# Earlier accumulating input transfers, four output slots, and a last half tile in two quarters

## The chip, the cores and the metric

The kernel runs on one core of a Trainium2 chip. The metric is the device time of one execution in microseconds. Seven executions of the kernel before gave a median of 156.28 us (155.72 to 157.04).

## The reference

The input x has 2048 rows and 640 columns in bf16. It is normalised per row; two branches read the result and their sum is added to x:

```python
x = A_x
xn = _layernorm(x, axis=-1)
return x + _A_ref(xn, A_w_r, A_w_i) + _B_ref(xn, B_w1, B_b1, B_w2, B_b2)
# _A_ref: irfft2(rfft2(xn) * (w_r + 1j * w_i)), over rows and columns
# _B_ref: gelu(xn @ w1 + b1) @ w2 + b2, inner width 1536
```

## The kernel before, in words

The rows are cut into 16 tiles (index c). Row 16p + c of x lies in partition p of tile c. Both branches are matrix products on TensorE. Branch A is a Fourier transform built from small tables: a forward part (tables gtab, etab, mtab), a filter multiplication on VectorE (L716, L721) with some small gathers into Zs (L731 to L738), and an inverse part (ntab, getab, htab). Branch B multiplies by W1, applies gelu on ScalarE into gT (L660), and multiplies by W2. All matmuls are issued by one helper, so they share line L477; copies out of PSUM share L484 (ScalarE) and L487 (VectorE).

The part that the change touches is the end. For a tile c, the output needs 24 matmuls of 320 columns for branch B (function second, two halves of the 640 columns), and two matmuls with htab for branch A, all summed in two PSUM banks. For the six tiles in STAGED (0, 2, 4, 6, 8, 10) the 24 matmuls run early; VectorE adds b2 and keeps the result as a float32 "kept sum" in the space of xnT (L795). For the other ten, ScalarE fills one of five float32 slots xo with b2 (L826), and the 24 and the two matmuls run together at the end. In both cases x itself is added by an accumulating DMA: GpSimd issues it at L828, and it adds a tile of x from DRAM to the kept sum or to the filled slot. VectorE then adds PSUM and that tile into a bf16 slot of ost (L840, one of three slots), and SP stores it (L842). Two tiles of branch A come from each inverse block of 16 matmuls with getab, whose result is copied to Wf (L484 or L487) and recombined by four VectorE instructions (L809, L814) before htab can be applied.

The order on each engine is not written by hand. The class Sched takes a list of operations with a cost, a priority, operands, "after" (a real dependency) and "gate" (only an order of planning: the operation is not planned before the gating one has started). It plans by greedy simulation; buffers taken from a Pool wait for the earlier users of their slot. For a DMA the plan adds a latency, of which lat is a part. sync() then turns dependencies into semaphore waits. Each engine executes its list in order, so an instruction that waits holds all behind it.

Two such rules sit on the input transfers: L826 has a gate, and L828 a dependency, on z_last (the last filter instruction) and on an output sum, os_ops[c - PACE] with PACE = 5. Tile 15, the last, is done in two halves, each with its own matmuls, sum and store.

Of the kernel before, what the change touches and what calls it, by code (L numbers as in the profile page):

```python
# [10 lines left out]
ALU = mybir.AluOpType  # L11

S = 2048
D = 640
F = 1536
H2 = 320
Q4 = 160
KP = 322
NFC = 12
# [104 lines left out]
PACE = 5  # L124
# [268 lines left out]
def bass_parallel_sum__spectral_gfnet__dense_activation_gelu__prompt_kernel(  # L393
# [13 lines left out]
    xv = A_x[0].rearrange("(p c) d -> p c d", c=16)  # L407
# [6 lines left out]
    K = Sched(nc, ["sp", "pe", "act", "dve", "pool"])  # L414
    with ExitStack() as es:
        def sb(name, shape, dtype=BF):
            return es.enter_context(nc.sbuf_tensor(name, shape, dtype))

        def view(t, off, dims):
            width = int(np.prod(t.shape[1:]))  # L420
            return bass.AP(tensor=t, offset=off, ap=[[width, 128]] + dims)
# [8 lines left out]
        htab = sb("htab", [128, 16, 128])  # L430
# [16 lines left out]
        TT = sb("T", [128, 11 * D])  # L447
        Zb = sb("Z", [128, 2, 4 * KP])
        Zs = sb("Zs", [128, 2, 2, 256])
        ost = sb("ost", [128, 3, D])  # L450
        xot = sb("xo", [128, 5, D], F32)
        PS = [es.enter_context(nc.psum_tensor(f"ps{i}", [128, 1024], F32)) for i in range(4)]

# [20 lines left out]
        def mms(lst):  # L474
            def f(e, _):
                for o_, lw, rh, st, sp_ in lst():
                    ins = e.matmul(o_, lhsT=lw, rhs=rh, start=st, stop=sp_)  # L477
                return ins
            return f
# [301 lines left out]
        def second(c, hs, fps, gate, done):  # L781
            part = list(gate)
            for f0 in range(0, NFC, 2):
                part = [K.op([("pe", 2 * len(hs) * mm_us(H2))], PRIO["fst" if done else "fin"] - c / 10, mms(lambda f0=f0: [
                    (ps(fps.slot + h, 0, H2), gT[:, fc, 128 * c:128 * c + 128], W2[:, fc, H2 * h:H2 * h + H2], fc == 0, done and fc == NFC - 1)
                    for fc in range(f0, f0 + 2) for h in hs]),
                    reads=B_w2s[f0 // 3:(f0 + 1) // 3 + 1] + [B_gT[block_of[c], fc] for fc in range(f0, f0 + 2)], writes=[fps], gate=part)]
            return part

        def halves(v):  # L790
            return v.rearrange("p (h n) -> p h n", n=H2)
        for i, c in enumerate(STAGED):
            fps, B_st2[c] = Buf(f"fst{c}", psum, 2, ZONE["fst"]), Buf(f"sum{c}")
            st_ops += second(c, (0, 1), fps, all_hps, True)
            K.op([("dve", dve_us(D))], 86, lambda e, _, i=i, fps=fps: e.tensor_tensor(  # L795
                out=halves(view(xnT, 2 * D * i, [[1, 2 * D]]).bitcast(F32)), in0=ps2(fps.slot, H2), in1=halves(b2bc[:]), op=ALU.add), reads=[fps, B_b2b], writes=[B_st2[c]], after=all_hps)
        for cp in range(8):
            yo, y2, yf = Buf(f"yo{cp}", p_yo), Buf(f"y2{cp}", p_y2), Buf(f"yf{cp}", p_yf)
            pr = PRIO["eps"] - cp / 5
            eps_ = [Buf(f"eps{cp}_{v}", psum, 2, ZONE["eps"]) for v in range(2)]  # L800
            K.op([("pe", FIVE)], pr, mms(lambda cp=cp, eps_=eps_: five(
                eps_, lambda g, n: V[:, (0, 2, 3, 1)[g], 2 * cp + n, :], lambda g, n: V[32 * g:32 * g + 32, 4, 2 * cp + n, :], getab)),
                reads=B_v + [B_ge], writes=eps_, gate=[fin_ops[2 * cp - 5]] if cp > 2 else [])
            for v in range(2):
                K.op([("act", act_us(640)), ("dve", dve_us(640))], pr,
                     copy(lambda v=v, yo=yo: view(Wf, YO + yo.slot * 2 * D + H2 * v, [[D, 2], [Q4, 2], [1, Q4]]),
                          lambda v=v, eps_=eps_: two(eps_[v])), reads=[eps_[v]], writes=[yo], after=filt_ops)
            for k, op in enumerate((ALU.add, ALU.subtract)):
                K.op([("dve", dve_us(D, 2))], pr + 2, lambda e, _, k=k, op=op, yo=yo, y2=y2: e.tensor_tensor(  # L809
                    out=view(Wf, Y2 + y2.slot * 2 * D + (H2 - 1) * k, [[H2, 4], [1 - 2 * k, Q4]]),  # L810
                    in0=view(Wf, YO + yo.slot * 2 * D, [[H2, 4], [1, Q4]]), in1=view(Wf, YO + yo.slot * 2 * D + Q4, [[H2, 4], [1, Q4]]), op=op),
                    port=True, reads=[yo], writes=[y2])
            for k, op in enumerate((ALU.add, ALU.subtract)):
                K.op([("dve", dve_us(D, 2))], pr + 3, lambda e, _, k=k, op=op, y2=y2, yf=yf: e.tensor_tensor(  # L814
                    out=view(Wf, YF + yf.slot * 2 * D + (D - 1) * k, [[D, 2], [1 - 2 * k, H2]]),
                    in0=view(Wf, Y2 + y2.slot * 2 * D, [[D, 2], [1, H2]]), in1=view(Wf, Y2 + y2.slot * 2 * D + H2, [[D, 2], [1, H2]]), op=op),
                    port=True, reads=[y2], writes=[yf])
            for n in range(2):
                c = 2 * cp + n
# [8 lines left out]
                K.op([("pool", 1.2)], 50, lambda e, _, c=c, xov=xov: e.dma_start(xov(0, D), xv[:, c, :], accum_op=ALU.add), reads=[xi], writes=[xo],  # L828
                     after=[z_last] + os_ops[max(c - PACE, 0):][:1], nbytes=163840, lat=1.0)
                part = []  # L830
                for hs in ((0, 1),) if c < 15 else ((0,), (1,)):
                    os_, fps = Buf(f"os{c}_{hs[0]}", p_os), Buf(f"fps{c}_{hs[0]}", psum, 2, ZONE["yps" if c in STAGED else "fps"])
                    a, b = H2 * hs[0], H2 * (hs[-1] + 1)
                    if c not in STAGED:
                        part = second(c, hs, fps, part + fin_gate(c), False)
                    fin_ops[c] = K.op([("pe", len(hs) * mm_us(H2))], PRIO["fin"] + 1 - c / 10, mms(lambda c=c, n=n, hs=hs, yf=yf, fps=fps: [
                        (ps(fps.slot + h, 0, H2), htab[:, c, :], view(Wf, YF + yf.slot * 2 * D + D * n + H2 * h, [[1, H2]]), c in STAGED, True) for h in hs]),
                        reads=[yf, B_h], writes=[fps], gate=part)
                    part = [fin_ops[c]]
                    os_ops.append(K.op([("dve", dve_us(H2 * len(hs)))], 95, lambda e, _, a=a, b=b, hs=hs, xov=xov, fps=fps, os_=os_: e.tensor_tensor(  # L840
                        out=halves(ost[:, os_.slot, a:b]), in0=ps2(fps.slot, H2)[:, hs[0]:hs[-1] + 1, :], in1=halves(xov(a, b)), op=ALU.add), reads=[fps, xi, xo], writes=[os_]))
# [33 lines left out]
```

## Time and profile before

| | |
|---|---|
| median of 7 executions | 156.28 us (155.72 to 157.04) |
| the profiled execution, its own time | 156.25 us |
| its span in the profile | 154.2 us |
| TensorE busy | 147.4 us (96%) |
| VectorE busy | 116.6 us (76%) |
| ScalarE busy | 86.6 us (56%) |
| GpSimd busy | 21.0 us (14%) |
| granted TensorE clock | 1.00 |

In the rows of the page, PE is TensorE's matmuls, PEld its weight loads, DVE VectorE, ACT ScalarE, POOL GpSimd and SP the engine that issues most transfers. A row of 40 digits cuts the span into slices of 3.85 us; a digit is the busy share in tenths. A wait is written "who <- whom: total us, times, longest us". A line of a timeline or of the chain gives its start in us from the beginning of the span, then its length. Matmuls overlap in the pipeline, so the distance from start to start is the better measure of what one costs.

### The profile page before, as it was taken

How to read it: one execution, taken by the hardware profiler on the slowest of the kernel's cores; microseconds unless marked ns; L12 is line 12 of the kernel's file. 1: busy time of each engine (PE TensorE's matmuls, PEld its weight loads, DVE VectorE, ACT ScalarE, POOL GpSimd, SP SyncE). 2: the span in 40 equal slices, each digit the busy share in tenths (PEclk: the TensorE clock that was granted, in tenths of full speed). 3: DMA queues.
4: the chain of work that ended last, by engine and by line, in shares of the span. 5: the costliest groups of instructions: out<-in, count | busy, mean ns of one | idle time of the engine just before them, and what ended most of it. 6: DMA issues, size and time to landing. Idle time of an engine off the chain costs nothing.

```text
span 154.2 us, 3728 instructions
## 1 busy us (share of the span) xinstructions
PE 147.4 (96%) x1525; PEld 101.0 (65%) x1533; DVE 116.6 (76%) x265; ACT 86.6 (56%) x177; POOL 21.0 (14%) x33
## 2 busy tenths in 40 slices
PE   5999999999999999999999999999999989999992
PEld 2499788999564545444557666766776757777770
DVE  3869999999974996798597699679579698762231
ACT  3199888988686788689786456349213053300000
POOL 1201121101200000000000000204643342210000
PEclk9999999999999999999999999999999999999999
DMA  4999928997999200413422000301999877942111
GB/s 105 330 362 395 292 70 171 208 171 110 159 176 226 34 0 4 122 9 128 128 30 104 0 4 0 66 23 54 215 265 271 225 195 191 240 97 75 55 43 43
DMA packets 20647, 20.80 MB, mean 135 GB/s; under 512 B 8088, under 2 KB 17304, under 8 KB 20504
## 3 DMA queue, kind: packets, MB, share of 16 engines
q1 hardware_dynamic: 18160, 15.30, 39.1%
q0 software_dynamic: 2304, 5.24, 15.3%
q8 instruction: 12, 0.20, 0.6%
q10 hardware_dynamic: 168, 0.04, 0.1%
q14 instruction: 3, 0.02, 0.1%
HBM read 13.69 MB, written 2.62 MB: 106 GB/s over the span
## 4 chain that ended last, share of the span: by engine, by line
PE 72%; DMA 12%; DVE 6%; SPq 2%; issue 2%; ACT 2%; POOL 1%; DVEq 0%; POOLq 0%; ACTq 0%
PE ps L477 72%; DMA XV<-in_A_x_dram 5%; DMA xnT<-in_A_x_dram 4%; DMA out_dram<-ost 3%; SPq L472 2%; DVE ost L840 2%; ACT Xb L484 1%; DVE stats L574 1%; ACT Wf L484 1%; DVE Wf L809 1%; POOL xo L828 1%; POOL xnT L828 1%; DVE Wf L487 0%; DVE T L593 0%; PE ps L602 0%
## 5 line engine op out<-in xcount | busy, mean ns | idle before, releaser
L477 PE MATMUL ps<-W,gT 128*128 128x320 bf16 x384 | 56.6, 299 | 0.5 <-DVE ost L840 0.4
L477 PE MATMUL ps<-xnT,W 128*128 128x256 bf16 (+2 forms) x412 | 55.4, 286 | 1.5 <-issue 0.6
L477 PEld LDWEIGHTS ps<-W,gT 128*128 128x128 bf16 x384 | 36.6, 98 | 15.8 <-DVE ost L840 1.2
L660 ACT ACTIVATE gT<-ps,b1col 128x256 bf16<-128x256 f32 (+2 forms) x84 | 40.0, 506 | 7.8 <-PE ps L477 5.3
L477 PEld LDWEIGHTS ps<-xnT,W 128*128 128x128 bf16 x420 | 34.7, 98 | 14.2 <-issue 1.3
L840 DVE TENSOR_TENSOR ost<-ps,xo 128x640 bf16<-128x640 f32 (+1 forms) x11 | 8.4, 764 | 12.5 <-PE ps L477 12.1
L484 ACT ACTIVATE Wf<-ps 128x640 bf16<-128x640 f32 x10 | 6.8, 701 | 18.9 <-PE ps L477 18.9
L574 DVE BATCH_NORM_STATS2 stats<-XV 128x6 f32<-128x320 bf16 x32 | 14.1, 469 | 2.5 <-DMA XV<-in_A_x_dram 2.4
L828 POOL DMA_DIRECT2D xnT<-in_A_x_dram x6 | 6.7, 1137 | 61.5 <-DVE Zs L486 57.0
L716 DVE TENSOR_TENSOR T<-Y,Wf 128x1288 bf16<-128x1288 bf16 x16 | 12.6, 828 | 1.0 <-ACT Y L484 0.4
L828 POOL DMA_DIRECT2D xo<-in_A_x_dram x10 | 10.4, 1088 | 19.3 <-DVE ost L840 15.8
L582 POOL TENSOR_TENSOR rstd<-ve,mhalf 128x2 f32<-128x2 f32 (+1 forms) x9 | 6.3, 703 | 33.0 <-DVE ve L581 33.0
L484 ACT ACTIVATE XV<-ps 128x640 bf16<-128x640 f32 x11 | 7.4, 703 | 5.0 <-PE ps L477 4.8
L484 ACT ACTIVATE Xb<-ps 128x640 bf16<-128x640 f32 x9 | 7.9, 896 | 3.7 <-PE ps L477 3.7
L487 DVE CAST Y<-ps 128x644 bf16<-128x644 f32 x8 | 6.6, 827 | 4.2 <-PE ps L477 4.0
L826 ACT ACTIVATE xo<-b2bc 128x640 f32<-128x640 bf16 x10 | 6.9, 734 | 3.3 <-DVE ost L840 3.3
L477 PE MATMUL ps<-etab,XW 128*128 128x160 bf16 (+1 forms) x128 | 8.6, 233 | 0.0
L477 PE MATMUL ps<-getab,XV 128*128 128x160 bf16 (+1 forms) x128 | 8.6, 233 | 0.0
L809 DVE TENSOR_TENSOR Wf<-Wf 128x640 bf16<-128x640 bf16 x16 | 7.2, 485 | 1.4 <-ACT Wf L484 1.3
L477 PEld LDWEIGHTS ps<-etab,XW 128*128 128x128 bf16 (+1 forms) x128 | 5.5, 95 | 3.8 <-DVE Y L487 0.7
L487 DVE CAST Xb<-ps 128x640 bf16<-128x640 f32 x7 | 6.2, 884 | 2.1 <-PE ps L477 2.1
L484 ACT ACTIVATE XW<-ps 128x640 bf16<-128x640 f32 x11 | 7.4, 700 | 0.5 <-PE ps L477 0.5
(49 smaller groups left out, 145.4 us busy)
## 6 DMA issues: line engine op xcount, KB each, us to landing
W<-in_B_w_dram SPq DMA_DIRECT2D x8, 480.0 KB, 4.5
xo<-in_A_x_dram POOLq DMA_DIRECT2D x10, 320.0 KB, 5.0
out_dram<-ost SPq DMA_DIRECT2D x15, 160.0 KB, 3.2
XV<-in_A_x_dram SPq DMA_DIRECT2D x7, 320.0 KB, 9.0
xnT<-in_A_x_dram POOLq DMA_DIRECT2D x6, 320.0 KB, 4.9
Wf<-in_A_w_r_dram SPq DMA_DIRECT2D x7, 160.5 KB, 4.4
Wf<-in_A_w_i_dram SPq DMA_DIRECT2D x7, 160.5 KB, 4.0
gtab<-c_G SPq DMA_DIRECT2D x1, 512.0 KB, 7.4
```

What stands on the lines that cost most here:

```text
L472: return K.op([(eng, cost)], 0, lambda e, _: e.dma_start(dst, src), reads=reads, writes=[buf], after=after, nbytes=nbytes, rate=rate)
L477: ins = e.matmul(o_, lhsT=lw, rhs=rh, start=st, stop=sp_)
L484: return e.activation(dst(), src(), ACT.Copy, scale=scale)
L487: return e.tensor_copy(dst(), src())
L574: K.op([("dve", 0.4)], 100 - c, lambda e, _, c=c, h=h: e.bn_stats(stats[:, c, 6 * h:6 * h + 6], view(XV, c * D + H2 * h, [[1, H2]])), read ...
L582: K.op([("pool", 0.75)], 100 - c, lambda e, _, a=a, b=b: e.tensor_tensor(out=rstd[:, a:b], in0=ve[:, a:b], in1=mhalf[:, 0:b - a], op=ALU.pow),
L660: K.op([("act", act_us(s1 - s0, 1))], pr + PRIO["gelu"], lambda e, _, s0=s0, s1=s1, fc=fc, hps=hps: e.activation(gT[:, fc, s0:s1], ps(hps. ...
L716: t_ops[pair].append(K.op([("dve", 0.05 + dve_us(4 * KP, 2))], pr, lambda e, _, k=k, Y=Y, TB=TB, pair=pair: e.tensor_tensor(out=view(TT, T ...
L809: K.op([("dve", dve_us(D, 2))], pr + 2, lambda e, _, k=k, op=op, yo=yo, y2=y2: e.tensor_tensor(out=view(Wf, Y2 + y2.slot * 2 * D + (H2 - 1 ...
L826: K.op([("act", act_us(640))], 30, lambda e, _, xov=xov: e.activation(xov(0, D), b2bc[:], ACT.Copy), reads=[B_b2b], writes=[xi], gate=[z_l ...
L828: K.op([("pool", 1.2)], 50, lambda e, _, c=c, xov=xov: e.dma_start(xov(0, D), xv[:, c, :], accum_op=ALU.add), reads=[xi], writes=[xo], aft ...
L840: os_ops.append(K.op([("dve", dve_us(H2 * len(hs)))], 95, lambda e, _, a=a, b=b, hs=hs, xov=xov, fps=fps, os_=os_: e.tensor_tensor(out=hal ...
```

## The change

The transfer at L828 loses its dependencies on z_last and on an earlier output sum: it waits only for the kept sum or the filled slot that it adds to. The filling at L826 keeps z_last as its gate alone. The planned latency of the transfer rises from 1.0 to 2.5. ost gets a fourth slot. Tile 15 is done as one half and two quarters of 160 columns; second and the loop take pieces (PSUM bank, first column, end column) instead of halves. The planner makes new orders for the end of each engine's list from this: on GpSimd the transfers of tiles 0, 2, 4 come first, then 1, 3, 5, 6, 7, 9, 8, and so on; TensorE's list differs from about 99 us on.

```diff
-        ost = sb("ost", [128, 3, D])
+        ost = sb("ost", [128, 4, D])
...
-        p_yo, p_y2, p_yf, p_xo, p_os = Pool(3), Pool(2), Pool(3), Pool(5), Pool(3)
+        p_yo, p_y2, p_yf, p_xo, p_os = Pool(3), Pool(2), Pool(3), Pool(5), Pool(4)
...
+        WHOLE = ((0, 0, H2), (1, H2, D))
+
+        def second(c, pcs, fps, gate, done):
+
             part = list(gate)
             for f0 in range(0, NFC, 2):
...
+                    (ps(fps.slot + k, 0, b - a), gT[:, fc, 128 * c:128 * c + 128], W2[:, fc, a:b], fc == 0, done and fc == NFC - 1)
+                    for fc in range(f0, f0 + 2) for k, a, b in pcs]),
...
                 if c not in STAGED:
                     K.op([("act", act_us(640))], 30, lambda e, _, xov=xov: e.activation(xov(0, D), b2bc[:], ACT.Copy), reads=[B_b2b], writes=[xi],
-                         gate=[z_last] + os_ops[max(c - PACE, 0):][:1])
-                K.op([("pool", 1.2)], 50, lambda e, _, c=c, xov=xov: e.dma_start(xov(0, D), xv[:, c, :], accum_op=ALU.add), reads=[xi], writes=[xo],
-                     after=[z_last] + os_ops[max(c - PACE, 0):][:1], nbytes=163840, lat=1.0)
+                         gate=[z_last])
+                K.op([("pool", 1.2)], 50, lambda e, _, c=c, xov=xov: e.dma_start(xov(0, D), xv[:, c, :], accum_op=ALU.add), reads=[xi], writes=[xo], nbytes=163840, lat=2.5)
                 part = []
-                for hs in ((0, 1),) if c < 15 else ((0,), (1,)):
-                    os_, fps = Buf(f"os{c}_{hs[0]}", p_os), Buf(f"fps{c}_{hs[0]}", psum, 2, ZONE["yps" if c in STAGED else "fps"])
-                    a, b = H2 * hs[0], H2 * (hs[-1] + 1)
+                for pcs in (WHOLE,) if c < 15 else (((0, 0, H2),), ((0, H2, H2 + Q4),), ((0, H2 + Q4, D),)):
+                    a, b = pcs[0][1], pcs[-1][2]
+                    os_, fps = Buf(f"os{c}_{a}", p_os), Buf(f"fps{c}_{a}", psum, len(pcs), ZONE["yps" if c in STAGED else "fps"])
...
-                    os_ops.append(K.op([("dve", dve_us(H2 * len(hs)))], 95, lambda e, _, a=a, b=b, hs=hs, xov=xov, fps=fps, os_=os_: e.tensor_tensor(
-                        out=halves(ost[:, os_.slot, a:b]), in0=ps2(fps.slot, H2)[:, hs[0]:hs[-1] + 1, :], in1=halves(xov(a, b)), op=ALU.add), reads=[fps, xi, xo], writes=[os_]))
+                    os_ops.append(K.op([("dve", dve_us(b - a))], 95, lambda e, _, a=a, b=b, xov=xov, fps=fps, os_=os_: e.tensor_tensor(
+                        out=ost[:, os_.slot, a:b] if b - a < D else halves(ost[:, os_.slot, :]), in0=ps(fps.slot, 0, b - a) if b - a < D else ps2(fps.slot, H2),
+                        in1=xov(a, b) if b - a < D else halves(xov(a, b)), op=ALU.add), reads=[fps, xi, xo], writes=[os_]))
```

In the changed file the lines of the input transfer, the output sum and its store are L831, L842 and L845; the filling is L829 and the kept sum L798.

More of the change, by code (lines that the diff above doesn't have):

```diff
@@ L778, in fin_gate @@
             return ([fin_ops[rest[i - AHEAD]]] if i >= AHEAD else st_ops[:]) + hps_ops[block_of[c]]
-        def second(c, hs, fps, gate, done):
+        WHOLE = ((0, 0, H2), (1, H2, D))
+        def second(c, pcs, fps, gate, done):
             part = list(gate)
             for f0 in range(0, NFC, 2):
-                part = [K.op([("pe", 2 * len(hs) * mm_us(H2))], PRIO["fst" if done else "fin"] - c / 10, mms(lambda f0=f0: [
-                    (ps(fps.slot + h, 0, H2), gT[:, fc, 128 * c:128 * c + 128], W2[:, fc, H2 * h:H2 * h + H2], fc == 0, done and fc == NFC - 1)
-                    for fc in range(f0, f0 + 2) for h in hs]),
+                part = [K.op([("pe", 2 * sum(mm_us(b - a) for _, a, b in pcs))], PRIO["fst" if done else "fin"] - c / 10, mms(lambda f0=f0: [
+                    (ps(fps.slot + k, 0, b - a), gT[:, fc, 128 * c:128 * c + 128], W2[:, fc, a:b], fc == 0, done and fc == NFC - 1)
+                    for fc in range(f0, f0 + 2) for k, a, b in pcs]),
                     reads=B_w2s[f0 // 3:(f0 + 1) // 3 + 1] + [B_gT[block_of[c], fc] for fc in range(f0, f0 + 2)], writes=[fps], gate=part)]
@@ L793, in bass_parallel_sum__spectral_gfnet__dense_activation_gelu__prompt_kernel @@
             fps, B_st2[c] = Buf(f"fst{c}", psum, 2, ZONE["fst"]), Buf(f"sum{c}")
-            st_ops += second(c, (0, 1), fps, all_hps, True)
+            st_ops += second(c, WHOLE, fps, all_hps, True)
             K.op([("dve", dve_us(D))], 86, lambda e, _, i=i, fps=fps: e.tensor_tensor(
@@ L834, in bass_parallel_sum__spectral_gfnet__dense_activation_gelu__prompt_kernel @@
                     if c not in STAGED:
-                        part = second(c, hs, fps, part + fin_gate(c), False)
-                    fin_ops[c] = K.op([("pe", len(hs) * mm_us(H2))], PRIO["fin"] + 1 - c / 10, mms(lambda c=c, n=n, hs=hs, yf=yf, fps=fps: [
-                        (ps(fps.slot + h, 0, H2), htab[:, c, :], view(Wf, YF + yf.slot * 2 * D + D * n + H2 * h, [[1, H2]]), c in STAGED, True) for h in hs]),
+                        part = second(c, pcs, fps, part + fin_gate(c), False)
@@ L838, in bass_parallel_sum__spectral_gfnet__dense_activation_gelu__prompt_kernel @@
+                    fin_ops[c] = K.op([("pe", sum(mm_us(hi - lo) for _, lo, hi in pcs))], PRIO["fin"] + 1 - c / 10, mms(lambda c=c, n=n, pcs=pcs, yf=yf, fps=fps: [
+                        (ps(fps.slot + k, 0, hi - lo), htab[:, c, :], view(Wf, YF + yf.slot * 2 * D + D * n + lo, [[1, hi - lo]]), c in STAGED, True) for k, lo, hi in pcs]),
                         reads=[yf, B_h], writes=[fps], gate=part)
                     part = [fin_ops[c]]
-                    os_ops.append(K.op([("dve", dve_us(H2 * len(hs)))], 95, lambda e, _, a=a, b=b, hs=hs, xov=xov, fps=fps, os_=os_: e.tensor_tensor(
-                        out=halves(ost[:, os_.slot, a:b]), in0=ps2(fps.slot, H2)[:, hs[0]:hs[-1] + 1, :], in1=halves(xov(a, b)), op=ALU.add), reads=[fps, xi, xo], writes=[os_]))
+                    os_ops.append(K.op([("dve", dve_us(b - a))], 95, lambda e, _, a=a, b=b, xov=xov, fps=fps, os_=os_: e.tensor_tensor(
+                        out=ost[:, os_.slot, a:b] if b - a < D else halves(ost[:, os_.slot, :]), in0=ps(fps.slot, 0, b - a) if b - a < D else ps2(fps.slot, H2),
+                        in1=xov(a, b) if b - a < D else halves(xov(a, b)), op=ALU.add), reads=[fps, xi, xo], writes=[os_]))
```

## The prediction

> **What bounds the kernel now.** I read the page first, then the waits, the chain in order of time, and the timelines of TensorE, VectorE and GpSimd around the places that these named. The page:
>
> ```profile
> span 154.2 us, 3728 instructions
> ...
> PE 147.4 (96%) x1525; PEld 101.0 (65%) x1533; DVE 116.6 (76%) x265; ACT 86.6 (56%) x177; POOL 21.0 (14%) x33
> ...
> DMA  4999928997999200413422000301999877942111
> ```
>
> TensorE is busy for 96% of the span, so only its gaps and its two ends can be shortened. The DMA row, slices counted from 0, is near zero in 22 to 27 (about 85 to 108 us) and seven to nine in 28 to 34: the accumulating input transfers come in a crowd. Who waits for whom:
>
> ```profile
> POOL xo L828 <- DVE ost L840: 15.8, 6, 7.8
> ...
> DVE ost L840 <- DMA xnT<-in_A_x_dram: 3.3, 3, 1.9
> ...
> PE ps L477 <- DVE ost L840: 0.4, 1, 0.4
> ```
>
> GpSimd sits for the output sum of an earlier tile before it issues an input (the wait that the change removes), VectorE for three late inputs; TensorE is charged with only 0.4 us. Of these only TensorE's own wait costs time. Its timeline gives it a place:
>
> ```profile
> 117.15 0.43 PE L477 MATMUL ps<-Wf,htab 128*128 128x320 bf16 x2
> 117.43 1.07 PE L477 MATMUL ps<-getab,XV 128*128 128x160 bf16 x16
> 118.33 0.43 PE L477 MATMUL ps<-Wf,htab 128*128 128x320 bf16 x2
> 118.83 3.43 PE L477 MATMUL ps<-W,gT 128*128 128x320 bf16 x24
> 122.10 0.43 PE L477 MATMUL ps<-Wf,htab 128*128 128x320 bf16 x2
> 122.38 1.07 PE L477 MATMUL ps<-getab,XV 128*128 128x160 bf16 x16
> 123.28 0.43 PE L477 MATMUL ps<-Wf,htab 128*128 128x320 bf16 x2
> 124.16 3.43 PE L477 MATMUL ps<-W,gT 128*128 128x320 bf16 x24 [0.44 <-DVE ost L840]
> ```
>
> Starts are what counts: 26 matmuls of 320 columns take 122.38 - 118.83 = 3.55 us, 136 ns each; an inverse block (getab) takes 0.90. Two matmuls should take 0.27, but 118.33 to 118.83 is 0.50 and 123.28 to 124.16 is 0.88: 0.23 and 0.61 us lost. The chain says why in the second case:
>
> ```profile
> 118.04 0.75 DVE ost L840
> 118.79 0.02 issue
> 118.80 4.14 DMA out_dram<-ost
> 122.94 0.33 issue
> 123.28 0.84 DVE ost L840
> 124.11 0.05 issue
> 124.16 27.00 PE ps L477 x216
> ```
>
> An output store took 4.14 us to land, the sum of tile 5 had to wait for its slot of the three in ost, and tile 7's matmuls for the PSUM that this sum frees. In the first case tile 3's sum (117.96 to 118.78 on VectorE) ran behind the recombinations of an inverse block that TensorE began at 114.06, in the midst of tile 3's matmuls. From 124.16 to the last matmul there is no gap.
>
> **What the Trainium skill says.** SBUF — State Buffer, "Who interferes with whom": a VectorE copy or tensor_scalar in a two-port mode and a GpSimd instruction lock each other out for a whole instruction; tensor_tensor does not lock out descriptor writing. The trace agrees with the second half: five issues from 106.13 on kept a pitch of 0.90 us beside pairs of L809/L814 that took 0.88 to 0.89 with or without them. For the first half there is one hint: the issue at 97.33 beside the last Zs copy (97.20 to 97.42) took 1.04 us instead of 0.88. DMA: Bandwidth & Descriptors, "Specifications": under 512 B a transfer is read, modified and written; nothing before shows a 320 B store. TensorE: Matmul & The Clock Gate, "LDWEIGHTS (loading the stationary operand)": a load takes columns/1.2 ns, 107 for 128; the trace has 98, yet full-height 160-column matmuls with their own loads start 69 to 70 ns apart, so the loads overlap.
>
> **The change part by part.**
>
> 1. Wait for z_last and an earlier output sum removed from L828. The six kept sums end at 86.5, 91.6, 96.2, 100.3 and later; GpSimd starts some 0.3 us after a release (as 119.07 after a sum ended 118.78). So the first issues move from 97.33 to about 86.8, 91.9 and 96.5, and the inputs of tiles 1, 3, 5, 6, 7, 9 follow between 97.4 and 103, before their old crowd at 106 to 117. Landing is 3.7 to 7.4 us in the old crowd; each input now lands over 5 us before its sum. VectorE's 3.3 us of input waits go.
>
> 2. ost with four slots. Tile 5's sum then waits for the store of tile 4's sum, issued near 113, not of tile 3's. The landing of 4.14 us has 9 us to hide in.
>
> 3. TensorE's order is replanned from 99 us. I followed it with the old durations. After the block that starts at 98.68 the same work remains up to tile 7's first matmul, in both orders: 140 matmuls of 320 columns x 0.136 = 19.04, six inverse blocks x 0.91 = 5.46: 98.68 + 24.50 = 123.18. The old kernel was there at 124.16: 0.98 of stalls, namely 0.09 at 101.6 (the second inverse block behind VectorE's copy of the first), 0.06 at 105.5, 0.23, 0.61. In the new order the 0.09 stays: first inverse block at 100.31, its copy on VectorE 101.42 to 102.24, the second could start at 102.31 but starts about 0.16 after that copy, 102.40. Then I looked for new waits. Tile 0's output matmul at 104.40: recombination ends 104.1. Tile 2's at 108.30: 108.0 (0.14 spare with the 0.16 of delay). Tile 4's at 111.83: 111.4. The inverse block of 114.06 now comes before all of tile 3's matmuls (at 112.92), so recombinations end by 117.2 and tile 3's sum follows its matmuls at once: 117.57 to 118.39, tile 5's first matmul due 118.55: 0.11 spare. Tile 5's sum: 122.29 to 123.11, tile 7's matmul due 123.27: 0.11 spare. So tile 7 starts at 123.27 instead of 124.16: **-0.89**. The spare 0.11 repeats in the later pairs, which had no gap before with the same pattern.
>
> 4. Fillings of xo (L826) lose their gates. On ScalarE they now stand ahead of the copies: the first runs while ScalarE idles (96.05 to 97.06); three run from 97.45 at a pitch of 0.63, and the copy behind them, on which the first inverse block waits, ends at 100.04, before 100.31. Later each filling waits for an output sum with an inverse copy queued behind it: tile 11's waits for tile 1's sum (113.94), so the copy at 114.03 starts at 114.61 and recombinations end near 117.2, for a block due 118.28. Covered by 1 us. Had sums waited for inputs again, this queue would pass it to TensorE.
>
> 5. Last half in quarters. 13 x 136 ns = 1.77 become 26 x 69.5 = 1.81: **+0.04**. The last sum has 160 columns: 640 take 0.82, 320 take 0.49, so 160 take 0.33: **-0.16**. The store has half the bytes; its 8 packets per DMA engine took 31 to 35 ns each, so at most -0.13, or a rise of about as much if a 320 B write is dearer. I take -0.03, bounds -0.13 and +0.3. The added store issue (0.33 on SP) falls 0.9 us before the last one and is hidden; unhidden it would cost 0.33.
>
> 6. GpSimd against the Zs copies. The issues at 91.9 and 96.5 (0.88 each), and the next one right behind it at 97.4, fall on VectorE's Zs copies at 92.4 and 97.06, which feed TensorE's blocks at 93.97 and 98.01. No run shows the copy as the loser. Bounds: 0, or all copies kept for a whole issue. One issue's rest (0.35) leaves about 0.1 to 0.25 on TensorE after spare. I take **+0.1**, since only GpSimd was seen to yield.
>
> Sum: -0.89 + 0.04 - 0.16 - 0.03 + 0.10 = -0.94. The profiled execution was 156.25 us for a span of 154.2; span 153.2, time 155.3. The median was 156.28, practically the same, so against it -0.6%.
>
> **The rivals.**
> - *A new wait replaces the old one* (inputs or GpSimd were never TensorE's limit; the spare of 0.11 is not there). For it: the margins are a tenth of a microsecond. Against: pairs after 124 ran this pattern without a gap. Most of 0.89 would come back: 156.0.
> - *Port lock, moderate:* the copies at 97.06 wait for two issues, about 0.9 late; 0.5 of spare at 98.01, then the queue of item 4 behind it: 0.4 to 0.5 lost, 155.7.
> - *Port lock, full; slower.* Place: the five Zs instructions between 92.4 and 98. Price: if each waits for a whole issue of 0.88, 4.4 us, less 0.5 spare and the gain of 1.04: 159.1. It decides from three such waits on (2.6 - 0.5 - 1.04 is a loss of 1.1). Against it: only three issues lie there, and queued copies need to lose once each.
> - *The store of 320 B rows is dear:* +0.3, 155.6.
> - *The change does nothing:* excluded for the order, since tile 5's wait for the late store is gone by construction.
>
> **How the numbers follow.** Forecast as summed (155.0 to 155.6): 0.56. Moderate lock or dear store (155.6 to 155.8): 0.17. New wait (155.8 to 156.5): 0.15. Full lock: 0.08; something unseen and slower: 0.04. About half a per cent, 0.78 us, is what a measurement tells from no change: faster means under 155.50, slower over 157.06. The forecast has four parts in five under 155.50, the mild cases a few hundredths more: 0.51 faster; 0.36 same; 0.13 slower. The range 154.9 to 156.4 leaves out the slower cases and a sliver of the rest.
>
> **What would show it.** Right: issues at L831 from about 87 us; the DMA row filled in slices 22 to 27 and thinner after 28; no VectorE wait for an input; TensorE 0.50 and 0.88 back at 0.27; last matmuls near 150.3; the last sum near 0.33 us. Wrong: TensorE gaps at 94 or 98 behind Zs with copies longer than 0.23 us (the lock), gaps behind L842 or ScalarE copies after 112 (a new wait), or more than 2.6 us from the last sum to the end (the store).

## The result, and the profile after

The median went from 156.28 us (33 runs) to 154.83 us (154.31 to 156.66, 13 runs): a ratio of 0.9902, 95% interval 0.9884 to 0.992. Ratios are formed over the fast executions alone (the 156.66 us is a slow one, with a granted clock of 0.989) and are not simply the quotient of the two medians. The profiled execution took 154.94 us, with a span of 152.8 us against 154.2. The direction was forecast; the gain was half as large again as the forecast: the median is 0.47 us below the predicted 155.3 and just below the low end of the range, 154.9.

The page of the kernel after, the lines that answer to the three of before:

```profile
span 152.8 us, 3751 instructions
...
PE 147.0 (96%) x1538; PEld 101.7 (67%) x1546; DVE 117.0 (77%) x267; ACT 86.3 (56%) x176; POOL 21.0 (14%) x33
...
DMA  3999936979989100224404043299865346551111
```

The DMA row, near zero in slices 22 to 27 before, now has two to four in 23 to 25 and nine in 26 and 27; in 28 to 34, where it had seven to nine, it has eight in the first and three to six in the others: the crowd of input transfers came forward. The waits of the kernel after:

```profile
POOL xnT L831 <- DVE xnT L798: 61.1, 6, 46.5
...
ACT xo L829 <- DVE ost L842: 19.1, 5, 5.8
POOL xo L831 <- ACT xo L829: 18.7, 6, 3.8
DVE ost L842 <- PE ps L477: 13.4, 12, 2.7
```

GpSimd waits only for what it adds to, the kept sum or the filled slot, and its first issues are these:

```profile
87.10 1.04 POOL L831 DMA_DIRECT2D xnT<-in_A_x_dram  x1 [46.48 <-DVE xnT L798]
92.14 0.88 POOL L831 DMA_DIRECT2D xnT<-in_A_x_dram  x1 [4.00 <-DVE xnT L798]
96.79 0.88 POOL L831 DMA_DIRECT2D xnT<-in_A_x_dram  x1 [3.77 <-DVE xnT L798]
```

The output sum waits for TensorE and for nothing else: the 3.3 us in which it waited for inputs are gone, and so is TensorE's wait for it. TensorE at the two places that the prediction named:

```profile
118.45 0.43 PE L477 MATMUL ps<-Wf,htab 128*128 128x320 bf16 x2
118.73 3.42 PE L477 MATMUL ps<-W,gT 128*128 128x320 bf16 x24
121.99 0.43 PE L477 MATMUL ps<-Wf,htab 128*128 128x320 bf16 x2
122.26 1.07 PE L477 MATMUL ps<-getab,XV 128*128 128x160 bf16 x16
123.17 0.43 PE L477 MATMUL ps<-Wf,htab 128*128 128x320 bf16 x2
123.44 2.74 PE L477 MATMUL ps<-W,gT 128*128 128x320 bf16 x19
```

The two distances that were 0.50 and 0.88 us are 118.73 - 118.45 = 0.28 and 123.44 - 123.17 = 0.27. The chain of work that ended last:

```profile
92.37 58.09 PE ps L477 x561
150.46 0.02 issue
150.48 0.32 DVE ost L842
```

One unbroken piece of TensorE from 92.37 us to the last sum. In the kernel before, the chain ended with

```profile
151.18 0.49 DVE ost L840
```

From the end of the last sum to the end of the span it is now 152.8 - 150.81 = 2.0 us; before it was 154.18 - 151.67 = 2.5 us. That last difference is what the forecast did not have.

The accounts of the two profiled executions, from the starts of TensorE's matmuls and the ends of the last sums and stores:

| term | forecast | measured |
|---|---|---|
| TensorE's gaps between 100 and 125 us | -0.89 | -0.98 |
| the last 26 matmuls of 160 columns instead of 13 of 320 | +0.04 | +0.04 |
| the last sum | -0.16 | -0.17 |
| the last store, issue to landing (1.58 to 1.50) | -0.03 | -0.08 |
| Zs copies beside GpSimd's issues | +0.10 | 0.00 |
| SyncE's stop at the end of its list | not in the sum | -0.43 |
| x loads 0.27 later at the start of this execution | none | +0.27 |
| sum | -0.94 | -1.35 |

The measured sum agrees with the difference of the spans, 152.8 - 154.2 = -1.4. It compares two single executions; how much its first row changes from one execution of the old order to another, the experiments show.

The row on SyncE comes from its own instruction records. SyncE closes the program by waiting for all output stores, up to two semaphores per wait instruction, and then takes a branch. Start in us and what it is, the last ones before the branch:

```
before (17 stores, 8 waits)              after (18 stores, 9 waits)
152.46  wait 6                           151.58  wait 6
152.53  wait 7                           151.65  wait 7
153.30  wait 8, on the last store        152.15  wait 8  (its store had landed at 151.42)
153.79  branch                           152.35  wait 9, on the last store
                                         152.41  branch
```

When nothing holds SyncE, one wait follows the next within 0.06 to 0.10 us. In the kernel before there are 0.49 us between the last wait, which ended when the last store had landed (153.28), and the branch: this is what the table calls SyncE's stop. In the kernel after the same 0.5 us lie between waits 7 and 8, while the last store is still under way (it landed at 152.33), and the branch follows the last wait by 0.06 us. Nothing in the diff speaks of this; the experiments had to say what moved it.

### The profile page after: what moved, and what is told of

It is laid out like the page before. It is cut to its first block, busy times and chain, and to the rows that moved or that the text cites. A ratio compares the mean times of both kernels' runs of the same rounds, so it can differ in the third digit from the quotient of the medians.

```text
span 152.8 us, 3751 instructions
## 1 busy us (share of the span) xinstructions
PE 147.0 (96%) x1538; PEld 101.7 (67%) x1546; DVE 117.0 (77%) x267; ACT 86.3 (56%) x176; POOL 21.0 (14%) x33
## 4 chain that ended last, share of the span: by engine, by line
PE 86%; DMA 5%; SPq 3%; DVE 2%; ACT 1%; issue 1%
PE ps L477 86%; DMA XV<-in_A_x_dram 5%; SPq L472 3%; ACT Xb L484 1%; DVE stats L574 1%; DVE T L593 0%; PE ps L602 0%; DVE xnT L487 0%; DVE ost L842 0%; DVE mv L576 0%
## 5 line engine op out<-in xcount | busy, mean ns | idle before, releaser
L477 PE MATMUL ps<-W,gT 128*128 128x320 bf16 (+1 forms) x396 | 56.6, 295 | 0.0
L477 PEld LDWEIGHTS ps<-W,gT 128*128 128x128 bf16 x396 | 37.4, 98 | 14.3 <-issue 0.8
L842 DVE TENSOR_TENSOR ost<-ps,xo 128x640 bf16<-128x640 f32 (+2 forms) x12 | 8.6, 713 | 12.4 <-PE ps L477 12.4
L829 ACT ACTIVATE xo<-b2bc 128x640 f32<-128x640 bf16 x10 | 7.1, 731 | 19.1 <-DVE ost L842 19.1
L831 POOL DMA_DIRECT2D xnT<-in_A_x_dram x6 | 5.4, 901 | 61.1 <-DVE xnT L798 61.1
L831 POOL DMA_DIRECT2D xo<-in_A_x_dram x10 | 9.5, 1042 | 18.7 <-ACT xo L829 18.7
```

Of the source, the lines that this page charges most:

```text
L842: os_ops.append(K.op([("dve", dve_us(b - a))], 95, lambda e, _, a=a, b=b, xov=xov, fps=fps, os_=os_: e.tensor_tensor(out=ost[:, os_.slot, ...
```

## The experiments

Two questions. **First, the TensorE gaps**: is it the early start of the inputs, the order of work, or the fourth slot of ost that closes them? **Second, the end**: why did 0.43 us go there? For the second there are two theories. A: the stop sits at a fixed place of SyncE's instruction list, 25 instructions from its first output store (17 stores and 8 waits in the kernel before, 18 stores and 7 waits in the kernel after); what counts is the one store more, not the quarters. B: the stop belongs to the end of the list, or to the last store. All ratios below are against runs of the kernel before on the same chip.

### One half left whole, quarters alone, slots alone, three slots

The first four were run together. e1_halves is the changed kernel with tile 15 in two halves again:

```diff
-                for pcs in (WHOLE,) if c < 15 else (((0, 0, H2),), ((0, H2, H2 + Q4),), ((0, H2 + Q4, D),)):
+                for pcs in (WHOLE,) if c < 15 else (((0, 0, H2),), ((0, H2, D),)):
```

> The changed kernel with tile 15 in two halves again; all else as changed. Theory 1 (the gaps of TensorE make the gain, the quarters bring only a shorter last sum, 0.17, and a slightly shorter store, 0.08, less 0.04 of matmuls): 0.2 us slower than the changed kernel, 155.05 us, ratio to before 0.992, and no gap of TensorE from 99 us on. Theory 2 (the end after the last sum, 2.5 us before and 2.0 us after, is 0.5 shorter because of the quarters): 155.5 us, ratio 0.995, with 2.5 us from the last sum to the end of the span.

155.53 us, ratio 0.9965 (0.9943 to 0.9986). The chain of this run:

```profile
92.02 58.13 PE ps L477 x548
150.16 0.02 issue
150.18 0.49 DVE ost L842
```

TensorE has no gap but one of 0.09 us, before the matmul at 102.33, and yet more than half of the gain is missing. From the end of the last sum, 150.67, to the end of the span it is 2.5 us again, and SyncE's branch comes 0.49 us after its last wait (152.32, 152.81), as before.

e2_quarters_only has the pieces of the changed kernel, with the waits of L826 and L828 and the three slots of before:

```diff
-                for hs in ((0, 1),) if c < 15 else ((0,), (1,)):
+                for pcs in (WHOLE,) if c < 15 else (((0, 0, H2),), ((0, H2, H2 + Q4),), ((0, H2 + Q4, D),)):
```

> The kernel before with tile 15 in a half and two quarters, nothing else. Theory 1: the gaps at 118 and 123 us stay, the end is 0.2 us shorter: 156.1 us, ratio 0.9987. Theory 2: 0.65 us shorter: 155.65 us, ratio 0.996, with 2.0 us from the last sum to the end.

155.36 us, ratio 0.9932 (0.991 to 0.9953). The part that the prediction priced at -0.15 us brought 0.81 us of median. Not all of that need be the quarters': in the profiled execution TensorE's gaps come to 0.19 us only, where the kernel before had 0.98 with the same waits. Its span ends 2.0 us after the last sum; the stop lies between wait 7 (152.49) and wait 8 (152.98), and the branch follows the last wait by 0.07 us.

e3_four_slots_only is the kernel before with four slots in ost:

```diff
-        ost = sb("ost", [128, 3, D])
+        ost = sb("ost", [128, 4, D])
...
-        p_yo, p_y2, p_yf, p_xo, p_os = Pool(3), Pool(2), Pool(3), Pool(5), Pool(3)
+        p_yo, p_y2, p_yf, p_xo, p_os = Pool(3), Pool(2), Pool(3), Pool(5), Pool(4)
```

> The kernel before with four slots of ost, nothing else. Theory 1: the gap of 0.61 us (tile 5's sum behind a store that lands late) goes, the gaps of 0.23, 0.09 and 0.06 stay: 155.7 us, ratio 0.996. Rival (the input that lands late holds that sum in any case): 156.2 us, ratio 1.0, with the gap still there and a VectorE wait for an input.

155.64 us, ratio 0.998 (0.9958 to 1.0002). Gaps of 0.84 us in all stay, against 0.98. The end of the chain of this run:

```profile
113.69 1.11 issue
114.81 5.10 DMA xnT<-in_A_x_dram
119.91 1.27 issue
...
123.74 0.75 DVE ost L843
124.53 27.00 PE ps L477 x216
```

No store stands in it. A late input does: the transfer into xnT took 5.10 us, the sum that uses it came after it, the recombinations on VectorE behind that, and the gap is still there. In this execution the slot was not the limit. The ratio lies between the two expectations and decides nothing: the interval holds both 0.996 and 1.0.

e4_three_slots is the changed kernel with three slots:

```diff
-        ost = sb("ost", [128, 4, D])
+        ost = sb("ost", [128, 3, D])
...
-        p_yo, p_y2, p_yf, p_xo, p_os = Pool(3), Pool(2), Pool(3), Pool(5), Pool(4)
+        p_yo, p_y2, p_yf, p_xo, p_os = Pool(3), Pool(2), Pool(3), Pool(5), Pool(3)
```

> The changed kernel with three slots of ost; the order of all engines stays as changed. Theory 1 (inputs moved forward leave the stores a quiet time, so that a store lands within 3 us and three slots suffice): as the changed kernel, 154.85 us, ratio 0.990. Rival (the fourth slot carries the 0.61): 155.45 us, ratio 0.9945, with a gap of TensorE before tile 7.

154.68 us, ratio 0.9906 (0.9874 to 0.9938): the changed kernel within its interval, with no TensorE gap. Once the inputs come early, the fourth slot brings nothing that shows. In the medians of this group the inputs' part is -0.64 us (e1), the quarters -0.81 (e2), both together -1.49 (e4): the two add up, within what the intervals allow.

### One store more, without quarters

e5_halves_18_stores is e1 with the store of tile 12 cut into two; SyncE issues 18 stores again, but there are no quarters:

```diff
-                    last.append(K.op([("sp", 0.35)], 0, lambda e, _, c=c, a=a, b=b, os_=os_: e.dma_start(ov[:, c, a:b], ost[:, os_.slot, a:b]), reads=[os_], nbytes=256 * (b - a)))
+                    for a_, b_ in ((a, b),) if c != 12 else ((0, H2), (H2, D)):
+                        last.append(K.op([("sp", 0.35)], 0, lambda e, _, c=c, a=a_, b=b_, os_=os_: e.dma_start(ov[:, c, a:b], ost[:, os_.slot, a:b]), reads=[os_], nbytes=256 * (b_ - a_)))
```

> The first experiment's kernel (tile 15 in halves) with tile 12's store cut into two stores of 320 columns, so that SP has 18 output stores as the changed kernel has, while the last sum and the last store are still 320 columns wide. Theory A (SP loses about 0.49 us at a fixed place of its list, 25 instructions from the first output store on; with 17 stores this falls behind the last wait, with 18 before the last store has landed): the branch follows the last wait by 0.06 us, not 0.49; 155.1 us, 0.43 below the first experiment, ratio 0.9935. Theory B (the narrow last store brings it): 0.49 us stays, 155.5 us, ratio 0.9965.

155.0 us, ratio 0.9921 (0.9895 to 0.9947), where e1 had 0.9965. The last sum is the 0.49 us one of e1. SyncE's records, beside those of e1:

```
e1 (17 stores)                           e5 (18 stores)
151.53  wait 7                           151.52  wait 7
152.32  wait 8, on the last store        152.00  wait 8
152.81  branch                           152.32  wait 9, on the last store
                                         152.38  branch
```

The last wait ends at 152.32 in both; the branch comes 0.49 us later in the one and 0.06 in the other. A second store in the middle of the output, off the chain, did that.

e6_480_160 has small pieces but 17 stores: tile 15 as 480 and 160 columns.

```diff
-                for pcs in (WHOLE,) if c < 15 else (((0, 0, H2),), ((0, H2, H2 + Q4),), ((0, H2 + Q4, D),)):
+                for pcs in (WHOLE,) if c < 15 else (((0, 0, H2 + Q4),), ((0, H2 + Q4, D),)):
```

> The changed kernel with tile 15 in two pieces of 480 and 160 columns: the last sum and store are as narrow as in the changed kernel, but there are 17 stores. Theory A: 0.49 us between the last wait and the branch again, 155.25 us, ratio 0.993. Theory B: 0.06 us, 154.8 us, ratio 0.990.

155.0 us, ratio 0.9933 (0.9912 to 0.9954). In the trace the 160-column piece does not remove the stop: last wait at 153.68, branch at 154.18, 0.50 us. Theory A again, and a narrow last store is not what removes the stop. The median is 0.25 us lower than A expected, which the interval (0.3 us to each side) covers.

e11_before_18_stores is the kernel before with nothing but tile 12's store cut in two; the edit is that of e5, made at L842 of the kernel before.

> The kernel before with tile 12's output store issued in two halves of the columns, so that SyncE issues one store more; nothing else changed. If SyncE's stop of 0.49 us sits at a fixed place of its instruction list: it moves ahead of the last wait, the branch comes 0.06 us after that wait, 155.8 us, ratio about 0.997. If the stop belongs to the end of the list: 0.49 us stays behind the last wait, 156.25 us, ratio about 1.0.

155.38 us, ratio 0.9958 (0.9935 to 0.9982): all that this edit does is to add a store, and the kernel is faster. The last wait is at 152.82, the branch at 152.89; the stop lies between wait 7 (152.02) and wait 8 (152.50). A holds in all five of e1, e2, e5, e6 and e11, and the profiles of all other runs agree with it; B fails in e2, e5 and e11, and as a matter of the last store's width in e6. Every run has 17 or 18 output stores, so the count of 25 rests on these two cases. The medians give the extra store somewhat more than the records do: -0.88 us here and -0.53 from e1 to e5, against 0.43 in the trace, which the intervals of the ratios include. In e11's profile the rest of the gain is TensorE's: its gaps sum to 0.51 us instead of 0.98, at places that lie ahead of tile 12's store, which is the only thing that the edit touches.

### Order, waits and slots apart

e7_new_order_old_waits is the changed kernel with every engine's new order kept, and the two old dependencies put back on the input transfers after the planning:

```diff
+                waits.append((os_ops[max(c - PACE, 0):][:1], K.op([("pool", 1.2)], 50, lambda e, _, c=c, xov=xov: e.dma_start(xov(0, D), xv[:, c, :], accum_op=ALU.add), reads=[xi], writes=[xo], nbytes=163840, lat=2.5)))
...
         K.schedule()
+        for old, o in waits:
+            o.deps = o.deps + [z_last] + old
```

> The order of all engines as in the changed kernel, but each input transfer waits again for the last filter instruction and for the output sum of five tiles before. If the waits are what costs: the inputs crowd again, VectorE waits for those of tiles 6 to 10, TensorE has gaps of 0.3 to 1 us in all between 112 and 130 us, 155.3 to 155.8 us, ratio 0.994 to 0.997. If the new order alone brings the gain: no gaps, 154.8 us, ratio 0.990.

155.7 us where the kernel before had 156.23, ratio 0.9984 (0.996 to 1.0007): by the times the inputs' part is lost, and some of the quarters' part with it, for e2 with the old order and the old waits has 0.9932. In the profile the quarters' part is whole (the branch follows the last wait by 0.07 us), so that loss is not explained. The chain:

```profile
106.68 0.82 DVE ost L842
...
107.80 3.58 DMA xnT<-in_A_x_dram
111.48 0.82 DVE ost L842
...
113.35 0.49 DVE Wf L817
113.89 38.45 PE ps L477 x341
```

An output sum releases an input transfer, that lands after 3.58 us, the next sum waits for it, and VectorE's recombination behind that sum keeps TensorE waiting for 0.72 us. So the removed waits matter, and not the order alone.

e8_before_again is the kernel before, once more, for the profile of another execution.

> The kernel before, unchanged, for a second profile. If the gaps of 0.23 and 0.61 us are the same in every execution: 0.98 us of stalls between 99 and 124 us again. If they hang on when a store or an input lands: a different sum, as in the two experiments on the old order, which had 0.2 and 0.8 us, and then the gain of the transfers differs from what one profile shows.

155.97 us. Its gaps sum to 0.96 us, but they lie otherwise: the 0.61 us before tile 7's matmuls is two gaps of 0.23 and 0.45. Its chain passes through an input where the first execution's passed through a store:

```profile
113.52 0.52 issue
114.04 6.42 DMA xnT<-in_A_x_dram
120.46 0.03 DVEq L376
```

Which of the crowded transfers is late differs from one execution to the next; with the same order and waits the gaps came to 0.84 us in e3, 0.51 in e11 and 0.19 in e2.

e9_old_order_no_waits is the counterpart of e7: the order of before on every engine, but the input transfers without the two dependencies, dropped after the planning:

```diff
+                free.append((c, K.op([("pool", 1.2)], 50, lambda e, _, c=c, xov=xov: e.dma_start(xov(0, D), xv[:, c, :], accum_op=ALU.add), reads=[xi], writes=[xo],
+                     after=[z_last] + os_ops[max(c - PACE, 0):][:1], nbytes=163840, lat=1.0)))
...
         K.schedule()
+        for _, o in free:
+            keep = [w for b in o.reads for w in b.writers]
+            o.deps = [d for d in o.deps if d in keep]
```

> Before's order of instructions on every engine, three slots and half tiles, but the accumulating input transfers of L828 no longer wait for the filter's last step and for the buffer's release (the dependencies are dropped after the planning, so the place in GpSimd's list stays). If the waits are what costs: the inputs of tile 6 and its neighbours land some 3 us earlier, the TensorE gaps between 100 and 125 us sum to about 0.3 us instead of 0.9, 155.7 us, ratio about 0.9965. If the place in the order is what counts: gaps about 0.9 us, 156.2 us, ratio about 1.0.

157.06 us, ratio 1.0059 (1.0037 to 1.008): neither expectation. It is slower than before. GpSimd's issues in this run:

```profile
86.40 1.04 POOL L828 DMA_DIRECT2D xnT<-in_A_x_dram  x1 [46.55 <-DVE xnT L795]
104.82 0.88 POOL L828 DMA_DIRECT2D xo<-in_A_x_dram  x1 [17.38 <-ACT xo L826]
105.37 1.22 POOL L828 DMA_DIRECT2D xnT<-in_A_x_dram  x1
```

The first input goes 11 us earlier; the second in GpSimd's list is one into xo, whose filling stands late in ScalarE's list, and GpSimd waits 17.38 us for it with all the others behind. Then nine of the inputs are issued in one go, by 112.9 us, without the old waits to spread them out. What that does, in the chain:

```profile
112.75 0.83 DVE ost L840
113.60 7.67 DMA out_dram<-ost
...
121.39 0.06 DVE ost L840
...
123.94 0.75 DVE ost L840
124.69 0.05 issue
124.74 27.00 PE ps L477 x216
```

An output store took 7.67 us to land, a sum waited for its slot, and TensorE's gaps sum to 2.0 us (0.09, 0.07, 0.46, 0.92, 0.46). That is the mechanism which the prediction had read out of the kernel before, and here the fourth slot should help.

e12_old_order_no_waits_4_slots is e9 with four slots in ost (the edit of e3); the orders are those of e9. "The run before it" in the expectation is e9.

> The kernel of the run before it in kind (before's order, the accumulating input transfers without the two extra waits), now with four slots in the output ring; every engine's order stays the same. That kernel's chain went through an output store that took 7.67 us to land among the crowded inputs, and a sum that waited 2.1 us for that store's slot. If the late store is what made it slower than before: VectorE no longer waits for a store, the TensorE gap of 0.92 us near 123 us goes, the gaps after 100 us sum to 1.0 us or less instead of 1.9, 156.1 us or less, ratio about 0.999. If the old order itself costs it: the gaps stay near 1.9 us, 157.0 us, ratio about 1.006.

155.51 us where the kernel before had 155.83, ratio 0.9987 (0.9964 to 1.0009), against 1.0059 for e9. VectorE's wait for the store (2.1 us in e9) is gone, the gap of 0.92 us is gone, and all gaps come to 0.3 us. In its chain the piece of TensorE that ends with the last matmul is whole again:

```profile
91.90 58.34 PE ps L477 x548
```

The late store is what made e9 slow. The gap in the ratios between e9 and e12, 0.7%, is 1.1 us, and the difference of their gaps in the two profiled executions is 1.7.

e10_wait_filter_only is the changed kernel with one wait left, that for the last filter step. With it the planner puts the inputs on GpSimd in the order of the tiles.

```diff
-                K.op([("pool", 1.2)], 50, lambda e, _, c=c, xov=xov: e.dma_start(xov(0, D), xv[:, c, :], accum_op=ALU.add), reads=[xi], writes=[xo], nbytes=163840, lat=2.5)
+                K.op([("pool", 1.2)], 50, lambda e, _, c=c, xov=xov: e.dma_start(xov(0, D), xv[:, c, :], accum_op=ALU.add), reads=[xi], writes=[xo], after=[z_last], nbytes=163840, lat=2.5)
```

> The changed kernel, but the accumulating input transfers still wait for the last step of the filter (no longer for a buffer). If it is enough that the inputs are not held back by the ring of buffers: a first input issued near 97 us, no TensorE gap after 100 us, 154.8 us, ratio about 0.990. If the early start, before the filter's end, is needed: gaps come back in the first tiles, 155.3 us or more, ratio 0.994 or more.

154.91 us, ratio 0.9918 (0.9886 to 0.995), not to be told from the changed kernel, and without a TensorE gap. Its first issues:

```profile
97.14 1.04 POOL L831 DMA_DIRECT2D xnT<-in_A_x_dram  x1 [57.00 <-DVE Zs L487]
97.85 1.24 POOL L831 DMA_DIRECT2D xo<-in_A_x_dram  x1
98.40 1.59 POOL L831 DMA_DIRECT2D xnT<-in_A_x_dram  x1
```

In the kernel before they were

```profile
97.33 1.04 POOL L828 DMA_DIRECT2D xnT<-in_A_x_dram  x1 [57.03 <-DVE Zs L486]
106.13 0.88 POOL L828 DMA_DIRECT2D xo<-in_A_x_dram  x1 [7.76 <-DVE ost L840]
```

The first transfer starts no earlier than there. The difference is the second: 97.85 instead of 106.13. The start at 87 us, which gives the change its name, isn't needed.

### The runs side by side

The last two columns are of the one profiled execution of each: the sum of TensorE's gaps from 99 us on, and the distance from TensorE's first matmul behind ScalarE's last copies into Xb (92.10 us in the kernel before, 92.37 in the kernel after) to the end of the span. The distance leaves out how late an execution reaches this place: that was between 91.66 and 93.66 us, a spread larger than the gain, in a part of TensorE's list that is the same in all of them.

| run | order | extra waits of the inputs | slots | tile 15 | stores | ratio | gaps, us | distance, us |
|---|---|---|---|---|---|---|---|---|
| before | old | both | 3 | halves | 17 | 1 | 0.98 | 62.08 |
| e8 | old | both | 3 | halves | 17 | | 0.96 | 62.09 |
| e3 | old | both | 4 | halves | 17 | 0.998 | 0.84 | 61.95 |
| e9 | old | none | 3 | halves | 17 | 1.0059 | 1.98 | 63.10 |
| e12 | old | none | 4 | halves | 17 | 0.9987 | 0.28 | 61.36 |
| e1 | new | none | 4 | halves | 17 | 0.9965 | 0.09 | 61.17 |
| e11 | old | both | 3 | halves | 18 | 0.9958 | 0.51 | 61.21 |
| e5 | new | none | 4 | halves | 18 | 0.9921 | 0.09 | 60.75 |
| e6 | new | none | 4 | 480, 160 | 17 | 0.9933 | 0.08 | 60.90 |
| e2 | old | both | 3 | quarters | 18 | 0.9932 | 0.19 | 60.65 |
| e7 | new | both | 4 | quarters | 18 | 0.9984 | 0.72 | 61.17 |
| e10 | new | filter's end | 4 | quarters | 18 | 0.9918 | 0 | 60.44 |
| e4 | new | none | 3 | quarters | 18 | 0.9906 | 0 | 60.43 |
| after | new | none | 4 | quarters | 18 | 0.9902 | 0 | 60.43 |

The distances show the two parts without the noise of the start: e1 to e5, one store more, is 0.42 us, and the three kernels with quarters and without a gap agree within 0.01. By distance e7 keeps 0.91 us of the gain, more than its ratio shows. The new order comes from two edits, the lifted gates and the higher planned latency, and no run takes these two apart.

No run was faster than the changed kernel by more than the intervals.

## Why the prediction was right or wrong

**Step 1, the inputs: right.** Issues were forecast at 86.8, 91.9 and 96.5; they came at 87.10, 92.14 and 96.79, and this execution runs 0.27 later from its start. VectorE's waits for inputs went. The crowd came forward, but each landing in it is not shorter: the input issued at 102.00 took 8.56 us to land, longer than any input of before. But nobody waits for it now; tile 6's input landed at 108.26, its sum began at 119.40. What the step did not see is that the early first issue is worth nothing (e10) and that the gain needs the new order as much as the lifted waits: either alone gives nothing that the times show, or a loss (e7, e12, e9).

**Step 2, the fourth slot: wrong for this kernel.** The prediction read the chain of one execution, found a store of 4.14 us in it and credited the slot with the 0.61 us behind it. Even in that execution VectorE stood for only 0.33 us at tile 5's sum (the chain's issue line at 122.94; by its record the store landed at 123.20, 4.4 us after its issue). The rest of the delay was there already, as tile 6's sum before it had waited 0.89 us for its input. Four slots alone left 0.84 us of gaps (e3), three slots in the changed kernel brought none back (e4). The store was one late landing of several; with the slot given, an input was the next to be late. Only where the inputs crowd still more does the slot decide (e9, e12).

**Step 3, TensorE's gaps: right in place, short by 0.09, and the size in part luck.** Forecast -0.89, measured -0.98. That the gaps before the matmuls of tiles 5 and 7 would close was right, and the spares of 0.11 held. But the 0.98 was the size of the gaps in one execution: five with the old order and the old waits had 0.98, 0.96, 0.84, 0.51 and 0.19 us, and the step had no term for that spread. The 0.09 at the second inverse block, which I kept, went for another reason. Its first weight load needs a copy of VectorE and one of ScalarE. In the nine profiled runs without the two quarters TensorE waits for VectorE's copy in an instruction of its own ahead of the load, and the first matmul starts 0.15 us after that copy ended (before: 101.71 to 101.86). In the five with the two quarters the load itself waits for it, and the matmul starts 0.06 us after it (after: 102.53 to 102.59). The diff does not speak of these two waits; why they change places is not shown.

**Step 4, the fillings on ScalarE: right.** No copy behind them kept TensorE waiting.

**Step 5, the last half in quarters: this is the step that failed.** Its three priced terms were good: 24 matmuls of 160 columns in 1.66 us, 69 ns each; the last sum 0.32; the store 0.08 shorter. Missing was a fourth term. The forecast took what lies between the last sum and the end, 2.51 us, as store and fixed rest, changed only by the store. In truth 0.49 us of it was SyncE's stop, and the added store, which the step had costed at nothing since it is issued 0.9 us before the last, moved that stop ahead of the last wait. It was worth -0.43 us in the records, shown by e5 and e11 without any quarter and by e6 with a quarter but no added store. Moreover the cases gave an unseen effect a chance only on the slow side (0.04), and so the range ended at 154.9. The Trainium skill's DMA: Bandwidth & Descriptors, "Specifications", has transfers under 512 B read, modified and written; on the 320 B rows here no price of that shows: 1.50 us to land against 1.58 for 640 B rows, and packets of 20 ns in the median against 34, a little more than half for half the bytes.

**Step 6, the port lock: did not happen.** The price of +0.10 came from the Trainium skill's SBUF — State Buffer, "Who interferes with whom", and from one issue of 1.04 us beside a Zs copy. In the kernel after the first issue, at 87.10, also took 1.04 us with no Zs copy near: the first issue took 1.04 us in every profile here, whatever ran beside it. The Zs copies beside issues, on VectorE:

```profile
92.67 0.23 DVE L486 TENSOR_SCALAR Zs<-Z 128x128 bf16<-128x128 bf16 x1
92.81 0.26 DVE L487 COPY Zs<-Z 128x128 bf16<-128x128 bf16 x1
...
97.33 0.38 DVE L487 COPY Zs<-Z 128x128 bf16<-128x128 bf16 x2
```

In the kernel before, with no issue beside it:

```profile
92.54 0.22 DVE L487 COPY Zs<-Z 128x128 bf16<-128x128 bf16 x1
```

A copy took 0.26 us against 0.22, and two in a row 0.38 against the 0.36 of those at 97.06 in the kernel before: at most 0.04 us of lock, and no gap of TensorE behind it.

**The rivals.** No new wait took the old one's place, no lock decided, the small store wasn't dear. The rival that a transfer becomes late all the same did not occur in the changed kernel, but e7 shows how near it is: with the old waits in the new order a gap of 0.72 us stays.

So the errors are -0.43 (stop), -0.10 (lock), -0.09 (the gap at the second inverse block) and -0.05 (store) against +0.27 from the later start. The medians moved by 1.45 us, the profiled executions by 1.31.

## What to carry to other kernels

Take the stretch from the last computed value to the end of the program apart, instruction by instruction on the engine that waits for the stores, before calling it fixed: here a fifth of it was a stop that one more store moved out of the way. A late landing found in the chain of one execution says that the transfers are crowded, not that this buffer is short; ask which landing is late next, and take a second profile before giving such a gap a size: five of the old order had 0.19 to 0.98 us. And an early release helps only if the queue in front of the instruction is free too: the order on the issuing engine, the filling ahead of it, the waits and the output slots have to be judged together.

## What the runs showed of the hardware that was not expected

SyncE stops for 0.48 to 0.50 us at one place of its instruction list: behind 25 of its instructions, counted from the first output store, in all 14 profiles. Whether it shows depends on where the last wait lies: with 17 stores the stop is behind the last wait and costs 0.43 us of time (0.49 less the 0.06 that the branch takes in any case), with 18 it is before it and costs nothing. No record in the traces names a cause, so the cause is left open. The DMA packets that the traces mark as instruction give none either: in the kernel before the nearest start at 141.95 and 154.42 us, with the stop from 153.30 to 153.79.

The start of a matmul behind two waits goes with which wait stands where: 0.06 us after the later of two copies when the weight load itself waits for that one, 0.15 us when an instruction of its own ahead of the load does. This is read off the second inverse block, 0.06 in five profiles and 0.15 in nine; no run was made to test it.

A late store can be a matter of its neighbours: a store of 160 KB landed in 1.8 us when alone and in 7.67 us among nine accumulating inputs, which themselves took up to 11.68 us (e9).
